# A new written order, and GpSimd compute operations that each wait for the one before

## The chip, the cores and the metric

One core of a Trainium2 chip runs the kernel. Its engines are TensorE (PE; its weight loads are listed as PEld), VectorE (DVE), ScalarE (ACT), GpSimd (POOL) and SyncE (SP, which here only issues transfers). The metric is the time of one execution in device microseconds. Before the change it is 179.48 us, the median of three runs from 178.18 to 181.58.

## The reference, cut to what matters

```
state = 0                                   # per batch (4) and head (8), 48 x 48
for t in range(768):
    cur    = (u * k[t]) outer v[t]
    y[t]   = r[t] @ (state + cur)
    state  = w * state + k[t] outer v[t]

x     = y as (4, 768, 384)
u     = x + real(fft(fft(x, axis=1), axis=2))
un    = (u - mean(u)) / sqrt(var(u) + 1e-6)   # over the 384 columns
out   = u + relu(un @ w_ch1) @ w_ch2          # 384 -> 1536 -> 384
```

## The kernel before, in words

The recurrence is done in 24 chunks of 128 time steps, six for each of the four batches. For a chunk, k and r are scaled with powers of w (`KR`, line 386 for one half, 389 for both at once), transposed on TensorE (line 410) and copied to `KRT` (lines 420, 421). Their product `PR` (432, 434) gives the diagonal term, the scores (444) are copied (`AC`, 451) and masked (`MA`: on GpSimd at 453, on VectorE at 456). `y` is then summed on TensorE (508, 514, 535) and leaves as `X` (543, 545). The state runs along the chunks (475, 488, 490).

When a batch has its six `X`, sums and differences of it are formed that fold the two transforms: `HH` and `XF` chunk by chunk in batch 0 (lines 558, 561, 567), `EO`, `HH` and `XF` for the whole batch in batches 1 to 3 (586, 594, 603). The first transform multiplies `XF` with a table (line 636), the second follows at 677. Then come `UF` (689), the statistics, the normalised `UB` (696 to 701) and its transpose `UNT`. The two matrix products of the last step run in eight halves of a batch: line 765 into `HT` (770 on ScalarE, 771 on VectorE), line 786 into `osb` (796), which is stored.

Nothing is scheduled when the kernel runs or is built. All steps stand in a list, and `ORDER` is a written sequence of their numbers; a suffix such as `.1` chooses among the engines on which a step may run, or leaves a step out. `emit` goes through that sequence, gives each new tile the buffer of its ring that was free longest, and issues the step. So the sequence sets, for every engine and for the transfer queues of SP and POOL, which instruction stands behind which. Among the steps are matmuls on a tile of zeros (line 272, and 366) whose results nobody uses; `ORDER` takes in as many as it names.

GpSimd issues its own transfers as well: the four parts of `wuc` (302), the two weight tables (840, 843) and part of the stores (799). They stand in its queue among its compute operations.

Of the kernel before, what the change touches and what calls it, by code (L numbers as in the profile page):

```python
# [9 lines left out]
AluOp = mybir.AluOpType  # L10
# [5 lines left out]
H = 8  # L16
S = 768
D = 48
# [43 lines left out]
class _Schedule:  # L62
# [12 lines left out]
    def emit(self, order):  # L75
        last = {}
        for k, (n, a) in enumerate(order):
            o = self.ops[n]
            for t in o["new"] + o["use"] + o["uses"][a]:
                last[t] = k  # L80
        held = {name: [-1] * len(tiles) for name, tiles in self.rings.items()}
        for k, (n, a) in enumerate(order):
            o = self.ops[n]
            for t in o["new"]:
                ends = held[t.ring]
                m = min(range(len(ends)), key=ends.__getitem__)
                assert ends[m] < k, (o["name"], t.ring)
                ends[m] = last[t]
                t.value = self.rings[t.ring][m] if t.view is None else t.view(self.rings[t.ring][m])
            fn = o["alts"][a][2]  # L90
            if fn is not None:
                fn()
# [78 lines left out]
def kernel(  # L171
# [19 lines left out]
    sch = _Schedule()  # L191
# [690 lines left out]
```

## Time and profile before

| what | value |
|---|---|
| median of three runs | 179.48 us (178.18 to 181.58) |
| the profiled execution | 177.02 us, span 175.3 us |
| TensorE busy | 157.2 us, 90% of the span |
| VectorE busy | 138.7 us, 79% |
| ScalarE busy | 108.4 us, 62% |
| GpSimd busy | 80.8 us, 46% |

The span runs from the first to the last instruction of the profiled execution; its own time is 1.72 us longer. Busy shares are means over stretches that have different limits, so the table by stretch among the rows below tells more than this one. A busy TensorE is not TensorE at its peak, since matmuls overlap.

### The profile page before, as it was taken

The page shows a single profiled execution, that of the slowest core. Times are in us where ns is not written, and L with a number is a line of the kernel's source. Part 1 is how long each engine was busy: PE and PEld are TensorE (multiplying, and loading weights), DVE is VectorE, ACT ScalarE, POOL GpSimd, SP SyncE. Part 2 cuts the span into 40 slices and gives each one's busy share as a digit, 9 for nine tenths or more (in the row PEclk, how much of TensorE's full clock was granted, in tenths as well). Part 3 has the DMA queues.
Part 4 walks back from the last instruction along what each step waited for, and adds up shares of the span by engine and source line. Part 5 has one row for each costly group of instructions (what it writes and reads, how often), then busy time and mean ns, then how long its engine had stood idle before and what let it go on. Part 6 is the DMA issues. An engine that isn't in the chain of part 4 may idle for free. (4 is left out here: it accounts for less than half of the span.)

```text
span 175.3 us, 4260 instructions
## 1 busy us (share of the span) xinstructions
PE 157.2 (90%) x1589; PEld 111.8 (64%) x1590; DVE 138.7 (79%) x314; ACT 108.4 (62%) x260; POOL 80.8 (46%) x120
## 2 busy tenths in 40 slices
PE   6348989829999979999999899999999999999992
PEld 1136667627777756677666478667676876666661
DVE  5487999999988979999979998868899775511632
ACT  2375889528868995578996266957735770275210
POOL 6606947693776640466974453473452121020110
PEclk9999999999999999999999999999999999999999
DMA  5999989799099999999999989999500043420132
GB/s 117 219 202 212 245 166 221 181 186 175 2 184 177 203 212 201 186 238 138 213 199 230 267 174 244 187 138 227 152 0 0 4 121 81 112 95 0 45 124 100
DMA packets 98118, 27.08 MB, mean 155 GB/s; under 512 B 94369, under 2 KB 96930, under 8 KB 98098
## 3 DMA queue, kind: packets, MB, share of 16 engines
q1 hardware_dynamic: 92912, 21.70, 63.2%
q0 software_dynamic: 2064, 4.53, 11.0%
q10 hardware_dynamic: 3122, 0.59, 2.1%
q8 instruction: 12, 0.20, 0.5%
q14 instruction: 8, 0.07, 0.1%
HBM read 19.77 MB, written 4.72 MB: 140 GB/s over the span
## 5 line engine op out<-in xcount | busy, mean ns | idle before, releaser
L765 PE MATMUL bank<-UNT,W 128*128 128x384 bf16 x288 | 54.4, 326 | 0.0
L786 PE MATMUL bank<-W,HT 128*128 128x384 bf16 x276 | 51.9, 326 | 0.9 <-DMA W<-in_moe_w_ch_dram 0.9
L770 ACT ACTIVATE HT<-bank 128x384 bf16<-128x384 f32 x68 | 30.6, 494 | 27.2 <-PE bank L765 27.0
L765 PEld LDWEIGHTS <-W 128*128 128x128 bf16 x288 | 30.6, 114 | 11.5 <-DMA UNT<-UB 0.2
L786 PEld LDWEIGHTS <-HT 128*128 128x128 bf16 x276 | 25.9, 98 | 15.7 <-DMA W<-in_moe_w_ch_dram 1.1
L453 POOL TENSOR_SCALAR_AFFINE_SELECT MA<-AC 128x512 bf16<-128x512 bf16 x25 | 17.3, 701 | 10.8 <-ACT AC L451 8.4
L796 DVE SCALAR_TENSOR_TENSOR osb<-bank,rstd,UF 128x384 f32<-128x384 f32 x23 | 13.9, 614 | 9.3 <-PE bank L786 9.1
L386 POOL TENSOR_TENSOR KR<-kr,wtab 128x384 bf16<-128x384 f32 x15 | 16.5, 1106 | 7.3 <-DMA kr<-in_r_dram 5.4
L771 DVE TENSOR_SCALAR HT<-bank 128x384 bf16<-128x384 f32 x28 | 15.0, 552 | 6.1 <-PE bank L765 6.0
L386 DVE TENSOR_TENSOR KR<-kr,wtab 128x384 bf16<-128x384 f32 x29 | 16.5, 586 | 3.1 <-ACT wtab L326 2.8
L451 ACT CAST AC<-bank 128x512 bf16<-128x512 f32 x25 | 14.2, 586 | 4.1 <-PE bank L444 2.0
L799 POOL DMA_DIRECT2D out_dram<-osb x11 | 6.3, 568 | 22.0 <-DVE osb L796 19.9
L636 PE MATMUL bank<-te_t,XF 128*128 128x193 bf16 x108 | 12.2, 247 | 4.5 <-DVE XF L567 3.8
L456 DVE TENSOR_TENSOR MA<-bank,mtri 128x512 bf16<-128x512 f32 x23 | 15.4, 683 | 0.7 <-PE bank L444 0.6
L708 ACT ACTIVATE tn_t<-UF,sm 128x384 bf16<-128x384 f32 x24 | 14.8, 617 | 0.2
L410 PE MATMUL bank<-ident,KR 128*128 128x128 bf16 x112 | 12.0, 251 | 3.0 <-DVE KR L386 2.8
L432 POOL TENSOR_TENSOR PR<-KRT 128x512 bf16<-128x512 bf16 x9 | 10.4, 1156 | 7.3 <-ACT KRT L420 4.1
L636 PEld LDWEIGHTS <-XF 128*128 128x128 bf16 x120 | 9.9, 97 | 5.7 <-DVE XF L567 4.0
L689 DVE SCALAR_TENSOR_TENSOR UF<-bank,X 128x384 f32<-128x384 f32 x22 | 11.6, 548 | 1.7 <-PE bank L677 1.7
L410 PEld LDWEIGHTS <-KR 128*128 128x128 bf16 x112 | 8.8, 113 | 5.8 <-issue 3.5
L523 DVE TENSOR_TENSOR TT<-V,bank 128x384 bf16<-128x384 bf16 x19 | 10.3, 544 | 2.6 <-PE bank L514 2.5
L543 DVE TENSOR_TENSOR X<-bank,TT 128x384 bf16<-128x384 f32 x18 | 9.6, 550 | 2.4 <-PE bank L535 2.4
(108 smaller groups left out, 263.8 us busy)
## 6 DMA issues: line engine op xcount, KB each, us to landing
kr<-in_k_dram SPq DMA_DIRECT2D x23, 192.0 KB, 4.2
kr<-in_r_dram SPq DMA_DIRECT2D x23, 192.0 KB, 4.4
vt<-in_v_dram SPq DMA_DIRECT2D x23, 192.0 KB, 4.3
out_dram<-osb SPq DMA_DIRECT2D x12, 192.0 KB, 1.9
out_dram<-osb POOLq DMA_DIRECT2D x11, 192.0 KB, 3.1
W<-in_moe_w_ch_dram POOLq DMA_DIRECT2D x2, 576.0 KB, 7.5
W<-in_moe_w_ch_dram POOLq DMA_DIRECT2D x3, 384.0 KB, 6.2
te_t<-te_c SPq DMA_DIRECT2D x1, 579.0 KB, 5.4
```

What stands on the lines that cost most here:

```text
L386: eng.tensor_tensor(out=o, in0=x, in1=y, op=AluOp.mult)
L410: nc.tensor.transpose(tps[s]()[:, p, :], KR()[:, s, p, :], ident)
L451: op(("AC", i, a), [("ACT", "AC", lambda: nc.scalar.copy(AC(), A_ps[a]())), ("NONE", "", None)], r=[("A", i)], w=[("AC", i, a)], new=[AC], ...
L453: op(("MA", i, a), [("POOL", "MA", lambda: nc.gpsimd.affine_select(out=MA[a](), in_=AC(), pattern=[[0, NP], [1, 128]], base=0, channel_mul ...
L456: ("DVE", "MA", lambda: nc.vector.tensor_tensor(out=MA[a](), in0=A_ps[a](), in1=mtri.unsqueeze(1).to_broadcast([128, NP, 128]), op=AluOp.m ...
L636: nc.tensor.matmul(fp()[:, par, :], lhsT=lhsT[:, g * CH:g * CH + 128], rhs=rhs, start=(nb == 0 and par == 0), stop=(nb == last and par == ...
L708: ("ACT", "SQ", lambda: nc.scalar.activation(out=squares, in_=UF()[:, j, :], func=Act.Square, scale=-float(DM), bias=sm()[:, j:j + 1], acc ...
L765: nc.tensor.matmul(hp(), lhsT=W1[:, dt, ft // 4 * 512 + ft % 4:(ft // 4 + 1) * 512:4], rhs=UNT()[:, :, dt, :], start=(dt == 0), stop=(dt = ...
L770: op(("HT", hf, ft), [("ACT", "HT", lambda: nc.scalar.activation(out=HT()[:, ft, :], in_=hp(), func=Act.Relu, scale=-1.0)), ("DVE", "HT", ...
L771: ("DVE", "HT", lambda: nc.vector.tensor_scalar(out=HT()[:, ft, :], in0=hp(), scalar1=-1.0, scalar2=0.0, op0=AluOp.mult, op1=AluOp.max))],
L786: nc.tensor.matmul(mo(), lhsT=HT()[:, ft, j * 128:(j + 1) * 128], rhs=W2[:, ft, :], start=(ft == 0), stop=(ft == 11))
L796: one(("osb", hf, j), "DVE", "osb", lambda: nc.vector.scalar_tensor_tensor(out=osb(), in0=mo(), scalar=rstd()[:, j:j + 1], in1=UF()[:, j, ...
```

## The change: what it does

`ORDER` is another sequence over the same steps, with other choices of engine. `emit` now hands every compute instruction that it issues on GpSimd (not its transfers) to `chain`, which makes it wait for the completion of the preceding compute instruction there. Three helper functions return the instruction that they make so that this can be done. Nothing else changes; from the steps' definitions on, line numbers are higher by 11.

```diff
-            fn = o["alts"][a][2]
+            eng, key, fn = o["alts"][a]
             if fn is not None:
-                fn()
+                made = fn()
+                if eng == "POOL" and not key.startswith("dma"):
+                    self.chain(made)
...
 ORDER = """
-152 15 159 158 28 150 160 46 151 174 155 164 8 165 173.1 196 193 202 32 34 199.1 205 203 153 208 176 181 200.1 154 182
+155 159 152 202 30 203 150 158 151 168 208 172 205 206 154 211 209 173 164 199.1 163 165 200.1 181.1 179 162 161 201.1
...
+    before = []
+
+    def chain(made):
+        if before:
+            tc.add_manual_dep(made.ins, before[-1].ins.name,
+                              mybir.DependencyInfo(mybir.DependencyClass.Sync, mybir.DependencyReason.DATA),
+                              reason="all cores of GpSimd done")
+        before.append(made)
+
+    sch.chain = chain
...
-            eng.tensor_tensor(out=o, in0=x, in1=y, op=AluOp.mult)
+            return eng.tensor_tensor(out=o, in0=x, in1=y, op=AluOp.mult)
...
-            eng.tensor_tensor(out=TT(), in0=V(), in1=x.unsqueeze(2).to_broadcast([128, H, D]), op=AluOp.mult)
+            return eng.tensor_tensor(out=TT(), in0=V(), in1=x.unsqueeze(2).to_broadcast([128, H, D]), op=AluOp.mult)
...
-                eng.tensor_copy(TR()[0:97, 2 * g:2 * g + 2, :], TT()[0:97, 2 * g:2 * g + 2, 384:0:-1])
+                return eng.tensor_copy(TR()[0:97, 2 * g:2 * g + 2, :], TT()[0:97, 2 * g:2 * g + 2, 384:0:-1])
```

On GpSimd 99 instructions now wait for GpSimd itself, where 11 did. The counts that change most, before and after: masks `MA` 25 and 31 on GpSimd, 23 and 17 on VectorE; `HT` 28 and 23 on VectorE, 68 and 73 on ScalarE; half products `KR` 15 and 17 on GpSimd, 29 and 25 on VectorE, with 2 and 3 whole ones there; matmuls on zeros 11 and 10.

The first place is GpSimd's queue while the last sums of batch 0 are formed, around the two transfers of the first weight table (`W`, the rows with DMA). Before:

```order
L567 TENSOR_TENSOR XF_100<-HH_99 128x196
L558 TENSOR_TENSOR HH_99<-X_142 128x192
L386 TENSOR_TENSOR KR_91<-kr_102,wtab_78 128x8x48
L567 TENSOR_TENSOR XF_100<-HH_99 128x2x98
L840 DMA W_88<-in_moe_w_ch_dram 128x3x768
L386 TENSOR_TENSOR KR_90<-kr_104,wtab_79 128x8x48
L432 TENSOR_TENSOR PR_126<-KRT_122 128x512
L840 DMA W_88<-in_moe_w_ch_dram 128x3x768
L386 TENSOR_TENSOR KR_92<-kr_105,wtab_77 128x8x48
L403 CAST V_117<-vt_109 128x384
```

And now:

```order
L578 TENSOR_TENSOR XF_100<-HH_99 128x2x98
L569 TENSOR_TENSOR HH_99<-X_142 128x192
L578 TENSOR_TENSOR XF_100<-HH_99 128x2x98
L851 DMA W_88<-in_moe_w_ch_dram 128x3x768
L578 TENSOR_TENSOR XF_100<-HH_99 128x2x98
L851 DMA W_88<-in_moe_w_ch_dram 128x3x768
L464 AFFINE_SELECT MA_132<-AC_128 128x512
L397 TENSOR_TENSOR KR_93<-kr_103,wtab_77 128x8x48
L666 COPY TR_147<-TT_145 97x768
L443 TENSOR_TENSOR PR_123<-KRT_121 128x512
```

Three `XF` now lie at the two transfers where one did, and the product `KR` and `PR` between the transfers are gone from there.

The second place is VectorE from the last `X` of batch 1 to the `XF` of batch 1 for which TensorE's first transform waits. Before:

```order
L543 TENSOR_TENSOR X_143<-bank_63,TT_139 128x384
L386 TENSOR_TENSOR KR_92<-kr_104,wtab_78 128x8x48
L543 TENSOR_TENSOR X_142<-bank_64,TT_141 128x384
L586 TENSOR_TENSOR EO_144<-X_143 128x768
L586 TENSOR_TENSOR EO_144<-X_143 128x384
L386 TENSOR_TENSOR KR_92<-kr_104,wtab_78 128x8x48
L586 TENSOR_TENSOR EO_144<-X_143 128x768
L586 TENSOR_TENSOR EO_144<-X_143 128x384
L594 TENSOR_TENSOR HH_99<-EO_144 128x2x2x192
L594 TENSOR_TENSOR HH_99<-EO_144 128x2x192
L594 TENSOR_TENSOR HH_99<-EO_144 128x2x2x192
L603 TENSOR_TENSOR XF_101<-HH_99 128x2x3x98 x4
```

And now:

```order
L597 TENSOR_TENSOR EO_144<-X_143 128x768
L534 TENSOR_TENSOR TT_141<-V_115,bank_66 128x384
L753 RECIPROCAL rstd_171<-rstd_171 128x3
L605 TENSOR_TENSOR HH_99<-EO_144 128x2x2x192
L554 TENSOR_TENSOR X_143<-bank_66,TT_141 128x384
L605 TENSOR_TENSOR HH_99<-EO_144 128x2x2x192
L397 TENSOR_TENSOR KR_93<-kr_104,wtab_78 128x8x48
L597 TENSOR_TENSOR EO_144<-X_143 128x384 x2
L605 TENSOR_TENSOR HH_99<-EO_144 128x2x192 x2
L614 TENSOR_TENSOR XF_101<-HH_99 128x2x3x98 x4
```

The two large `EO` and one `HH` now stand ahead of the last `X` of the batch. On TensorE there are 45 matmuls of line 786 between that chunk's sum `y` and the first transform before, and 27 (now line 797) after; at the same place of batch 2 there are 45 of lines 765 and 786 before and 39 after.

## Rows read from the trace of the kernel before

**Rows 1.** The page: busy time of each engine over the span.
```profile
PE 157.2 (90%) x1589; PEld 111.8 (64%) x1590; DVE 138.7 (79%) x314; ACT 108.4 (62%) x260; POOL 80.8 (46%) x120
```

**Rows 2.** Busy time by stretch: bounds and length, engines, granted clock, DMA share, GB/s.
```profile
35.00:40.00 5.00, 1.87 (x26) 1.72 (x24) 5.00 (x5) 1.49 (x4) 4.70 (x6) 1.00 1.11 189
...
60.00:65.00 5.00, 4.06 (x60) 2.79 (x59) 4.07 (x9) 4.85 (x11) 2.66 (x5) 1.00 1.02 189
...
100.00:105.00 5.00, 4.40 (x38) 3.43 (x39) 4.91 (x12) 2.49 (x5) 2.28 (x2) 1.00 0.94 185
...
120.00:125.00 5.00, 4.88 (x72) 3.43 (x70) 3.75 (x9) 3.87 (x11) 1.78 (x3) 1.00 1.00 238
...
165.00:170.00 5.00, 5.00 (x35) 3.21 (x34) 1.97 (x5) 1.76 (x5) 1.08 (x2) 1.00 0.21 79
```

**Rows 3.** Timeline of PE: start, length, instruction, idle before it and its releaser.
```profile
38.16 0.26 PE L636 MATMUL bank<-te_t,XF 128*128 128x193 bf16 x1 [3.13 <-DVE XF L567]
```

**Rows 4.** Timeline of DVE, 32 to 38 us: an undisturbed XF and a long one.
```profile
32.21 0.25 DVE L567 TENSOR_TENSOR XF<-HH 128x196 bf16<-128x196 bf16 x1
...
34.45 3.18 DVE L567 TENSOR_TENSOR XF<-HH 128x196 bf16<-128x196 bf16 x1
```

**Rows 5.** Timeline of POOL, 34 to 38 us.
```profile
34.23 0.80 POOL L840 DMA_DIRECT2D W<-in_moe_w_ch_dram  x1
35.05 1.00 POOL L386 TENSOR_TENSOR KR<-kr,wtab 128x384 bf16<-128x384 f32 x1
36.00 1.15 POOL L432 TENSOR_TENSOR PR<-KRT 128x512 bf16<-128x512 bf16 x1
```

**Rows 6.** Timeline, 125.7 to 128.8 us: POOL with DVE's PR between.
```profile
125.78 0.82 POOL L523 TENSOR_TENSOR TT<-V,DE 128x384 bf16<-128x384 bf16 x1
126.29 0.59 DVE L432 TENSOR_TENSOR PR<-KRT 128x512 bf16<-128x512 bf16 x1
126.77 0.63 POOL L453 TENSOR_SCALAR_AFFINE_SELECT MA<-AC 128x512 bf16<-128x512 bf16 x1 [0.17 <-ACT AC L451]
...
127.36 0.50 POOL L403 CAST V<-vt 128x384 bf16<-128x384 f32 x1
127.94 0.83 POOL L523 TENSOR_TENSOR TT<-V,DE 128x384 bf16<-128x384 bf16 x1
```

**Rows 7.** Timeline at the start: DVE's icol and the last of POOL's six memsets.
```profile
2.56 2.07 DVE L304 CAST icol<-icol_i 128x3 f32<-128x3 int32 x1 [1.23 <-POOL icol_i L288]
...
4.28 0.32 POOL L310 MEMSET KR<- 128x256 bf16 x1
```

**Rows 8.** Timeline, 91 to 101 us: PE, then DVE.
```profile
97.83 2.11 PE L786 MATMUL bank<-W,HT 128*128 128x384 bf16 x12
100.47 1.74 PE L636 MATMUL bank<-te_t,XF 128*128 128x193 bf16 x15 [0.53 <-DVE XF L603]
...
94.73 4.35 DVE L594 TENSOR_TENSOR HH<-EO 128x768 bf16<-128x768 bf16 x3
99.18 1.62 DVE L603 TENSOR_TENSOR XF<-HH 128x588 bf16<-128x588 bf16 x4
```

**Rows 9.** Timeline of DVE, 65 to 73 us, then of PE at 71 us.
```profile
65.31 1.02 DVE L543 TENSOR_TENSOR X<-bank,TT 128x384 bf16<-128x384 f32 x2 [1.03 <-PE bank L535]
...
67.18 0.82 DVE L586 TENSOR_TENSOR EO<-X 128x768 bf16<-128x768 bf16 x2
...
69.12 1.56 DVE L594 TENSOR_TENSOR HH<-EO 128x768 bf16<-128x768 bf16 x4
70.71 1.92 DVE L603 TENSOR_TENSOR XF<-HH 128x588 bf16<-128x588 bf16 x4
...
71.26 2.61 PE L786 MATMUL bank<-W,HT 128*128 128x384 bf16 x15
```

**Rows 10.** The page: costliest groups, busy, mean ns of one, idle before.
```profile
L453 POOL TENSOR_SCALAR_AFFINE_SELECT MA<-AC 128x512 bf16<-128x512 bf16 x25 | 17.3, 701 | 10.8 <-ACT AC L451 8.4
...
L386 POOL TENSOR_TENSOR KR<-kr,wtab 128x384 bf16<-128x384 f32 x15 | 16.5, 1106 | 7.3 <-DMA kr<-in_r_dram 5.4
```

123 rows, old and new, of the table ORDER are left out of this document.

## The prediction

> **What bounds the kernel now.** The page comes first: TensorE is busy for 157.2 of 175.3 us, far more than any other engine [rows 1], so time can only come out of its idle 18 us, or be lost by adding to them. The table by stretch says where those are. From 45 us on it is busy in practically every microsecond (5.00 of 5 us, as in the stretch from 165 to 170) [rows 2]; before that it is VectorE that is full (5.00 of 5 us from 35 to 40) while TensorE has 1.87. So up to about 45 us the kernel goes at the pace of VectorE and of what it waits for, and afterwards at TensorE's.
>
> The timeline of TensorE names the largest gap: 3.13 us in the first transform of batch 0, ended by an `XF` of VectorE [rows 3]. From 45 to 170 us three stretches are not full and lack 0.94, 0.60 and 0.12 us [rows 2], 1.7 in all; 0.53 of it is for `XF` of batch 2 [rows 8].
>
> Why was `XF` late? Undisturbed it takes 0.25 us, but one took 3.18 [rows 4]. Beside it GpSimd issues a transfer and does a `KR` and a `PR`; the long `XF` ends at 37.63, after `PR` has ended at 37.15 [rows 5]. GpSimd's `KR` and `PR` overlap: 35.05 + 1.00 is 36.05, and `PR` starts at 36.00. VectorE stood through both. The same is seen twice more: the little `icol` took 2.07 us and ended at 4.63, just after the last memset of GpSimd's run, at 4.60 [rows 7]; three `HH` took 4.35 us [rows 8], against 1.56 us for four [rows 9]. Where GpSimd paused for 0.17 us (126.60 to 126.77) a waiting `PR` got through: it ended at 126.88, and GpSimd's next instruction kept its 0.63 us [rows 6].
>
> **The change part by part.** All sums are against the profiled execution, 177.02 us.
>
> *The wait on GpSimd.* Its price shows where `TT` needs the `V` cast directly before it: `V` ends at 127.86, `TT` starts at 127.94, a gap of 0.08 us [rows 6], where neighbours otherwise overlap by 0.05 [rows 5]. So 0.13 us for each pair that stood back to back. With 99 waits, that is at most 12.9 us on GpSimd and at least nothing, since its other waits cover the rest. Its own work grows by about 8 us: six masks at 0.70 and two `KR` at 1.11 make 6.4 [rows 10], and the remaining exchanges some 1.5. From 80.8 us it comes to between 89 and 102, up to 58% of the span. Behind a waiting instruction on that queue stand masks that `y` needs, `UB`, and transfers. After 45 us TensorE has other work in its order to cover that. Before 45 us GpSimd gives sums and masks to a stretch without cover; some 27 waits there are 0 to 3.5 us. I take 0.5, near the low end, because GpSimd's masks had 10.8 us of idle time before them anyway, 8.4 of it waiting for ScalarE's copy [rows 10]. **+0.5 us (0 to +3.5).**
>
> *The last sums of batch 0.* Up to the last `XF` of batch 0 VectorE has nearly the same list of instructions in both orders, by number and kind; so mainly its delays can change. What stood between the two transfers, `KR` and `PR`, is replaced by one `XF` that GpSimd itself does, and the instructions after the second transfer now have a pause between them. The delay of 2.93 us (3.18 less 0.25) [rows 4] should shrink to about one GpSimd instruction, 1.0 to 1.2 us [rows 5]: 1.7 less. Against it, if the pause of 0.08 us lets nobody in, nothing is gained; if it works as at 126.6, all 2.9 are. I take the middle, since the pause that was seen to work was twice as long. **-1.7 us (-2.9 to 0).** The next thing late would then be GpSimd's own `XF`, which waits behind a weight transfer of 0.80 us.
>
> *The start.* `icol` can gain up to 1.9 us, as GpSimd's memsets no longer form one run. But VectorE now has more memsets ahead of what the first matmul needs, and the first `KR` is made in one piece, from two tables instead of one at a time: about 1.0 us later relative to the tables. **0 us (-0.9 to +1.0).** Three of the six early matmuls on zeros also go. The granted clock reads 1.00 in all stretches [rows 2], TensorE does not bound this stretch, and I set 0, with +1 at the outside.
>
> *Ahead of the first transforms of batches 1 and 2.* Batch 1: from the last `y` to the transform TensorE has 27 table matmuls instead of 45. Fifteen take 2.45 us (2.61 less the tail that overlaps) [rows 9], so 27 take 4.4, and with four transposes and two groups of scores 5.3 us. VectorE has, from the last `X`: `X` 0.5, one large `HH` 0.5, `KR` 0.5, two small `EO` 0.6, two small `HH` 0.6, four `XF` 1.6 to 1.9 [rows 8, 9]: 4.3 to 4.6 us. Slack 0.7. Batch 2: 39 matmuls, 6.3 us, against `X` 0.5, four `EO` 1.6, four `HH` 1.6, a reciprocal 0.1, four `XF` 1.6 to 1.9: 5.4 to 5.7. Slack 0.6. Each bears one short delay by GpSimd, not two. Before, batch 2 had 45 matmuls, lost about 3 us on `HH`, and 0.53 us of that reached TensorE [rows 8]. Of the 1.7 us that were idle after 45 us I expect 0.3 at each of these two places and 0.5 elsewhere. **-0.6 us (-1.3 to +3.7).**
>
> *The rest.* VectorE loses about 5 us of work (six masks, five `HT`), which after 45 us nobody waits for while TensorE is full: 0. TensorE's own work is unchanged but for a few matmuls: 0. At the end two stores move to GpSimd, hidden by matmuls that still follow: 0 to +0.5.
>
> The sum: 0.5 - 1.7 + 0 - 0.6 = -1.8, so 175.2 us for an execution like the profiled one. The median shown is 2.46 us above that execution; I carry the difference along: **177.7 us**.
>
> A rule that speaks against part of this: the Trainium skill, page "SBUF — State Buffer", section "Who interferes with whom", says that a VectorE instruction with two SBUF inputs and a GpSimd instruction that reads SBUF exclude each other, and that the later one is held until the first has finished, thus through one instruction. By that rule the wait on GpSimd would free VectorE of nothing, and what the second term gives would come from the moved rows alone. Rows 4 and 5 differ from it: VectorE was held past the end of a first instruction and through a second.
>
> **The rivals.**
>
> *The pause works everywhere (faster).* Every wait of VectorE ends with the GpSimd instruction during which it began. For it: three long holds end exactly with GpSimd's runs [rows 4, 5, 7, 8]. Against: the pause is 0.08 us, only 0.17 is seen to work, and transfers are not chained, so a run of transfer and compute keeps its form. Then -2.9 at the sums, -0.9 at the start, -1.3 later and nothing lost: -5.1, a median of 174.4.
>
> *GpSimd sets the pace up to 45 us (no change).* It already has 4.70 of 5 us from 35 to 40 [rows 2]; the waits and the added `KR` and masks cost some 4.9 us there, of which 2 to 3 reach the first normalised rows. With the other terms, 2.5 - 1.7 - 0.6 = +0.2: 179.7.
>
> *The thin cover breaks (slower).* In batches 1 and 2 VectorE's `HH` or `XF` meet a run of GpSimd as at 94.73 [rows 8]: 3.1 us each time, less 0.7 and 0.6 of slack, so 4.9 us of TensorE idle. For it: GpSimd has `KR` for the next batch in its queue there. Against: these are now chained. With no gain at batch 0, 0.5 for the waits, 0.5 of other idle, and the old 1.7 gone, the sum is +4.2: 183.7. It decides from the second such run on; a single one gives no change.
>
> *The long hold was not GpSimd's doing,* and the wait changes nothing for VectorE: then only the price of the wait and the later places count, 0.5 - 0.6 = -0.1: 179.4.
>
> **How the numbers follow.** Two per cent, about what a measurement of this kernel can tell from no change (its three runs spread over 1.9%), is 3.6 us: faster is under 175.9, slower over 183.1. Chances: the forecast 0.40, all pauses work 0.24, GpSimd sets the pace 0.13, no effect on VectorE 0.10, thin cover 0.13. The forecast's own bounds reach a little below 175.9 and a little of the first rival stays above it, so faster 0.26; slower is the last rival with a bit of the unknown start, 0.14; within 2% the remaining 0.60. The range reaches down to the first rival's 174.4 and up to 182.0, which leaves out most of the slower case and the best end of the faster one.
>
> **What would show it right or wrong.** Right: the idle time ahead of batch 0's first transform falls from 3.13 us to 1 to 2; no VectorE instruction is held through two chained GpSimd instructions; GpSimd's neighbours stand 0.08 us apart; idle time of TensorE from 45 us to its last matmul is near 1.1 us (before: 1.7). Wrong: a long `XF` or `HH` beside chained instructions (the pause lets nobody in), idle TensorE of over 1 us ahead of the transforms of batches 1 or 2 (cover), or TensorE waiting for GpSimd's `XF`, masks or `UB` before 45 us (pace). Should the first matrix product begin later than 47 us, the start or GpSimd was mis-sized.

## The result and the profile after

The changed kernel takes 173.35 us (median of four runs, 172.38 to 173.67), the kernel before 179.21 us beside it (four runs, 178.18 to 181.58). The ratio is 0.968, with a 95% interval from 0.962 to 0.975: faster. A second comparison, below, gave 0.976 (0.973 to 0.980). Ratios are meant for undisturbed executions, without those that are over 1.5% longer than the shortest of their kernel; medians and ranges have all of them. Forecast were 177.7 us, in a range from 174.4 to 182.0; the result lies below the range.

The profiled execution of the changed kernel takes 173.32 us with a span of 171.6: 3.70 us less than before. Its page answers to [rows 1]: less work for VectorE, more for GpSimd, TensorE nearly as before.

```profile
PE 156.2 (91%) x1591; PEld 111.5 (65%) x1591; DVE 127.8 (74%) x310; ACT 109.7 (64%) x259; POOL 92.3 (54%) x128
```

The table by stretch answers to [rows 2], with three more stretches:

```profile
20.00:25.00 5.00, 3.80 (x60) 2.96 (x60) 4.99 (x10) 4.69 (x12) 3.99 (x7) 0.82 1.02 197
25.00:30.00 5.00, 4.49 (x64) 3.31 (x63) 4.96 (x13) 4.35 (x9) 3.82 (x5) 0.83 1.00 253
35.00:40.00 5.00, 4.93 (x68) 3.79 (x67) 5.00 (x11) 4.22 (x10) 4.68 (x6) 1.00 1.03 167
40.00:45.00 5.00, 3.47 (x54) 2.69 (x53) 3.82 (x12) 3.90 (x11) 4.43 (x7) 1.00 1.05 192
60.00:65.00 5.00, 5.00 (x45) 3.30 (x44) 2.99 (x9) 3.79 (x11) 1.87 (x3) 1.00 1.42 151
100.00:105.00 5.00, 5.00 (x46) 3.92 (x43) 3.61 (x11) 3.74 (x8) 3.23 (x4) 1.00 1.06 208
120.00:125.00 5.00, 5.00 (x56) 3.60 (x55) 4.90 (x11) 3.41 (x10) 4.70 (x7) 1.00 0.37 112
```

From 35 to 40 us TensorE has 4.93 us of work where it had 1.87; the three later stretches that were short are full. New is a hole from 40 to 45 us, and a granted clock of 0.82 and 0.83 from 20 to 30.

At the last sums of batch 0, VectorE answers to [rows 4] and GpSimd to [rows 5]:

```profile
34.49 0.26 DVE L578 TENSOR_TENSOR XF<-HH 128x196 bf16<-128x196 bf16 x1 [0.73 <-POOL XF L578]
34.67 0.99 DVE L397 TENSOR_TENSOR KR<-kr,wtab 128x384 bf16<-128x384 f32 x1
```
```profile
33.94 0.52 POOL L578 TENSOR_TENSOR XF<-HH 128x196 bf16<-128x196 bf16 x1
34.40 0.79 POOL L851 DMA_DIRECT2D W<-in_moe_w_ch_dram  x1
35.20 0.96 POOL L464 TENSOR_SCALAR_AFFINE_SELECT MA<-AC 128x512 bf16<-128x512 bf16 x1
36.23 1.00 POOL L397 TENSOR_TENSOR KR<-kr,wtab 128x384 bf16<-128x384 f32 x1
37.30 1.05 POOL L666 COPY TR<-TT 97x768 bf16<-97x768 bf16 x1
38.43 1.16 POOL L443 TENSOR_TENSOR PR<-KRT 128x512 bf16<-128x512 bf16 x1
```

`XF` takes 0.26 us, and TensorE has no gap ahead of or in the first transform (before 3.13 us, [rows 3]). GpSimd's neighbours stand 0.07 and 0.08 us apart (36.23 + 1.00 to 37.30, 37.30 + 1.05 to 38.43). VectorE's `KR`, which starts while the second transfer is issued (34.40 to 35.19), takes 0.46 us more than its next one (0.53 us).

At the start, VectorE's `icol` (before [rows 7]) and TensorE's first transposes:

```profile
1.66 0.39 DVE L315 CAST icol<-icol_i 128x3 f32<-128x3 int32 x1
```
```profile
8.47 1.90 PE L421 MATMUL bank<-ident,KR 128*128 128x128 bf16 x16 [3.74 <-DVE KR L400]
```

The transposes began at 9.18 us before. And the hole, on TensorE:

```profile
43.06 0.33 PE L776 MATMUL bank<-UNT,W 128*128 128x384 bf16 x1
44.70 1.49 PE L776 MATMUL bank<-UNT,W 128*128 128x384 bf16 x8 [1.31 <-DMA W<-in_moe_w_ch_dram]
```

One matmul of the first matrix product runs, then 1.31 us are lost to a weight transfer. Its end, 44.70, is where the second transfer (issued at 34.40) lands after 10.3 us, though these products need columns of the first alone, which had landed at 41.3. This fits a dependency that is taken over the whole stretch of memory that a transfer spans: with both halves interleaved in `W1[dt][F]` the second one spans the columns of `dt` 1 and 2 too, and the one matmul that ran reads `dt` 0, which lies ahead of that stretch. The thirds and halves below test it.

How far the changed kernel is ahead, by the useful matmul columns that TensorE still has to do (at each time of the old execution, when the new one had as many left):

```
old execution, us     20    36    40    46    48    68    100   140   last matmul   span
new one earlier by    1.2   1.1   4.2   4.7   2.6   3.7   3.1   4.1   4.1           3.7
```

So 1.1 us from the start, 3.1 at the gap, 0.5 up to 46, 2.1 lost again around the weight transfer, 1.5 gained later, 0.4 lost behind the last matmul. A second trace of the changed kernel (at the end of the weight transfers, below) differs from this one by up to 0.7 us on the way, so smaller differences between two traces tell little.

### The profile page after: what moved, and what is told of

Its sections match the earlier page's. It is cut to its first block, busy times and chain, and to the rows that moved or that the text cites. A ratio compares the mean times of both kernels' runs of the same rounds, so it can differ in the third digit from the quotient of the medians.

```text
span 171.6 us, 4305 instructions
## 1 busy us (share of the span) xinstructions
PE 156.2 (91%) x1591; PEld 111.5 (65%) x1591; DVE 127.8 (74%) x310; ACT 109.7 (64%) x259; POOL 92.3 (54%) x128
## 4 chain that ended last, share of the span: by engine, by line
PE 58%; DMA 12%; POOL 11%; DVE 6%; issue 6%; ACT 4%; POOLq 0%; DVEq 0%; ACTq 0%
PE bank L776 24%; PE bank L797 21%; DMA W<-in_moe_w_ch_dram 6%; POOL KR L397 3%; DMA wuc<-in_w_dram 3%; DMA KRT<-KR 3%; PE bank L647 2%; PE bank L688 2%; PE bank L455 2%; POOL MA L464 2%; PE bank L546 2%; POOL UB L712 1%; DVE TT L534 1%; PE bank L823 1%; POOL PR L443 1%
## 5 line engine op out<-in xcount | busy, mean ns | idle before, releaser
L781 ACT ACTIVATE HT<-bank 128x384 bf16<-128x384 f32 x73 | 33.1, 495 | 29.0 <-PE bank L776 28.8
L464 POOL TENSOR_SCALAR_AFFINE_SELECT MA<-AC 128x512 bf16<-128x512 bf16 x31 | 21.4, 690 | 14.3 <-issue 6.9
L810 POOL DMA_DIRECT2D out_dram<-osb x14 | 8.0, 571 | 28.2 <-DVE rstd L753 18.1
L397 POOL TENSOR_TENSOR KR<-kr,wtab 128x384 bf16<-128x384 f32 x17 | 19.1, 1124 | 6.8 <-ACT wtab L337 4.1
L462 ACT CAST AC<-bank 128x512 bf16<-128x512 f32 x31 | 17.7, 593 | 6.2 <-PE bank L455 2.8
L782 DVE TENSOR_SCALAR HT<-bank 128x384 bf16<-128x384 f32 x23 | 12.3, 551 | 7.9 <-PE bank L776 5.9
L719 ACT ACTIVATE tn_t<-UF,sm 128x384 bf16<-128x384 f32 x21 | 13.1, 623 | 1.2 <-DVE UF L700 1.1
L534 DVE TENSOR_TENSOR TT<-V,bank 128x384 bf16<-128x384 bf16 x21 | 11.4, 548 | 2.7 <-ACT AC L462 1.2
L455 PE MATMUL bank<-KRT 64*128 64x128 bf16 x192 | 10.2, 229 | 2.0 <-ACT KRT L431 0.6
L467 DVE TENSOR_TENSOR MA<-bank,mtri 128x512 bf16<-128x512 f32 x17 | 11.4, 682 | 0.6 <-PE bank L455 0.6
```

The source lines that it names most:

```text
L397: return eng.tensor_tensor(out=o, in0=x, in1=y, op=AluOp.mult)
L455: nc.tensor.matmul(A_ps[a]()[:, p, :], lhsT=KRT()[rows, 0, p, :], rhs=QT(p, rows), start=(p == 0), stop=(p == NP - 1), skip_group_check=True)
L462: op(("AC", i, a), [("ACT", "AC", lambda: nc.scalar.copy(AC(), A_ps[a]())), ("NONE", "", None)], r=[("A", i)], w=[("AC", i, a)], new=[AC], ...
L464: op(("MA", i, a), [("POOL", "MA", lambda: nc.gpsimd.affine_select(out=MA[a](), in_=AC(), pattern=[[0, NP], [1, 128]], base=0, channel_mul ...
L534: return eng.tensor_tensor(out=TT(), in0=V(), in1=x.unsqueeze(2).to_broadcast([128, H, D]), op=AluOp.mult)
L719: ("ACT", "SQ", lambda: nc.scalar.activation(out=squares, in_=UF()[:, j, :], func=Act.Square, scale=-float(DM), bias=sm()[:, j:j + 1], acc ...
```

## The experiments

**The order alone, and the wait alone.** The first leaves the two lines out that call `chain`; the second has the changed code with the old `ORDER`.

```diff
-                if eng == "POOL" and not key.startswith("dma"):
-                    self.chain(made)
```

> The new order without the waits on GpSimd. Theory one (the waits let VectorE in, and the order uses that): without them GpSimd's neighbours overlap again, VectorE is held through two or three of them in several places, its holds together grow by some 4 to 8 us, and the time goes back by 1.5 to 3 us, to 175 to 177 us. Rival (the order alone does it, the waits only cost): the time stays at 173.4 or falls by up to 1 us, since 88 waits at 0.08 to 0.13 us leave GpSimd; VectorE's holds stay as they are.

> The old order with the waits. Theory one: the XF that took 3.18 us in the old kernel takes 1.2 to 2.0 us, the gap ahead of batch 0's first transform falls from 3.13 to 1 to 2 us, the run of three HH of 4.35 us shrinks to about 2.5, and the time falls by 1.5 to 3 us, to 176 to 178 us. Rival (the order alone): XF stays above 2.7 us, or another instruction is held instead, and the time stays within 1 us of 179.2 or rises by the price of the waits before 45 us, 0.5 to 3.5 us.

Order alone: 175.59 us, ratio 0.985 (0.978 to 0.992). Wait alone: 175.99 us, ratio 0.987 (0.975 to 1.000). By these ratios each gives about 1.4% and both together 3.2 (2.4 in the second comparison). That they simply add is not shown, for the wait alone scatters as the kernel before does: its four executions take 173.42, 175.01, 176.96 and 178.62 us, and its ratio evidently has the long ones in it, for the two shorter ones are 2.3% below the kernel before. The shortest has the trace, and is as short as the changed kernel: its transposes begin 1.32 us earlier than before, its gap is 1.45 us, and its last matmul ends 3.6 us earlier (4.1 in the changed kernel). TensorE and VectorE of the wait alone:

```profile
35.25 0.26 PE L648 MATMUL bank<-te_t,XF 128*128 128x193 bf16 x1 [1.45 <-DVE XF L579]
```
```profile
91.53 3.96 DVE L606 TENSOR_TENSOR HH<-EO 128x768 bf16<-128x768 bf16 x3
```

The run of three `HH` (4.35 us, [rows 8]) stays long, where 2.5 was expected: GpSimd's two `KR` there alternate with transfers, which aren't chained. In the changed kernel `HH` of this size take 0.55 us on average.

That the order does it alone is out: its four executions (175.2 to 176.0) lie above all ten of the changed kernel's (172.4 to 173.9). At the start it needs no waits: its `icol` takes 0.39 us as well, and its transposes begin at 8.28. It is up to 0.5 us ahead of the changed kernel from 28 to 34 us, which may be the price of the waits, and 2.5 behind it at 38: without the waits the loss moves one instruction on. VectorE, GpSimd and TensorE of the order alone:

```profile
37.49 2.64 DVE L395 TENSOR_TENSOR KR<-kr,wtab 128x384 bf16<-128x384 f32 x1
```
```profile
36.83 0.81 POOL L664 COPY TR<-TT 97x768 bf16<-97x768 bf16 x1
37.62 1.14 POOL L441 TENSOR_TENSOR PR<-KRT 128x512 bf16<-128x512 bf16 x1
38.73 0.98 POOL L395 TENSOR_TENSOR KR<-kr,wtab 128x384 bf16<-128x384 f32 x1
```
```profile
40.19 0.62 PE L419 MATMUL bank<-ident,KR 128*128 128x128 bf16 x8 [2.02 <-DVE KR L395]
```

`XF` is free, but the next `KR`, 0.53 us in the changed kernel at this place, is held for 2.1 us through three overlapping instructions, and TensorE stands for 2.02 us. Behind that gap the granted clock falls to 0.50, half speed (stretches of 1 us, columns as before):

```profile
42.00:43.00 1.00, 1.00 (x9) 0.83 (x7) 1.00 (x4) 0.00 (x0) 0.58 (x1) 0.50 1.18 216
43.00:44.00 1.00, 1.00 (x8) 0.92 (x7) 0.53 (x4) 0.74 (x3) 0.05 (x1) 0.50 1.10 220
```

**One wait, and the waits of the start.** Old order; `chain` waits at one place alone (`PR` behind `KR`, between the two transfers), or among GpSimd's first twelve compute instructions.

```diff
-        if before:
+        if len(before) == 31:                 # the one wait
+        if before and len(before) < 12:       # the waits of the start
```

> The old order with a single wait: GpSimd's PR between the two weight transfers waits for the KR ahead of it. Theory one (a pause of 0.08 us is enough for VectorE): the XF that took 3.18 us ends with KR, about 1.7 us, the gap of 3.13 us ahead of batch 0's first transform falls by 1.2 to 1.5 us, and the time falls by as much, a ratio of 0.992. Rival (the pause is too short, or the next held instruction takes back the gain): XF stays over 2.7 us or a KR or HH of VectorE behind it is held by PR for as long; the gap stays above 2.7 us and the ratio is 1.00.

> The old order with the waits only among GpSimd's first twelve compute instructions (memsets and masks of the start), none later. Theory one (the pauses let icol through): icol takes 0.4 to 0.5 us instead of 2.07, the first transposes begin at 7.9 instead of 9.18 us, and all later events up to the long XF are 1.3 us earlier; the XF is held as before (2.9 us); the time falls by 1.3 us, a ratio of 0.993. Rival (the start is waited for by nobody, because the loads land later anyway): icol is short, but from 20 us on the lead is under 0.3 us and the ratio is 1.00.

One wait: 175.06 us, ratio 0.988 (0.983 to 0.993), by the ratios as much as all 84 added ones give in that order (0.987), though the wide interval of those leaves room for more. VectorE, GpSimd and TensorE of this kernel, to be held against [rows 3 to 5]:

```profile
33.87 1.74 DVE L579 TENSOR_TENSOR XF<-HH 128x196 bf16<-128x196 bf16 x1
```
```profile
33.66 0.80 POOL L852 DMA_DIRECT2D W<-in_moe_w_ch_dram  x1
34.47 1.00 POOL L398 TENSOR_TENSOR KR<-kr,wtab 128x384 bf16<-128x384 f32 x1
35.55 1.24 POOL L444 TENSOR_TENSOR PR<-KRT 128x512 bf16<-128x512 bf16 x1
```
```profile
35.84 0.26 PE L648 MATMUL bank<-te_t,XF 128*128 128x193 bf16 x1 [1.38 <-DVE XF L579]
```

A pause of 0.08 us (34.47 + 1.00 to 35.55) lets VectorE in: `XF` falls from 3.18 to 1.74 us, the gap from 3.13 to 1.38. The transfer ahead of `KR` isn't chained, and through these two `XF` is still held. By the Trainium skill, page "SBUF — State Buffer", section "Who interferes with whom", as the forecast read it, the wait would free VectorE of nothing; here it freed it of 1.44 us, so the measurement decides against that reading.

The waits of the start: 176.58 us, ratio 0.995 (0.991 to 0.999). VectorE and TensorE:

```profile
2.56 0.47 DVE L316 CAST icol<-icol_i 128x3 f32<-128x3 int32 x1 [1.23 <-POOL icol_i L300]
```
```profile
7.86 1.03 PE L422 MATMUL bank<-ident,KR 128*128 128x128 bf16 x8 [1.91 <-DVE KR L398]
...
36.69 0.26 PE L648 MATMUL bank<-te_t,XF 128*128 128x193 bf16 x1 [3.13 <-DVE XF L579]
```

`icol` takes 0.47 us instead of 2.07, the transposes begin 1.32 us earlier, and the lead is still 1.47 us at 36.69, where the old gap of 3.13 us ends. Then some 0.8 of it are lost: here the clock falls behind the gap, which it didn't in the first profile.

```profile
38.00:39.00 1.00, 1.00 (x9) 0.94 (x8) 1.00 (x3) 0.23 (x2) 0.27 (x1) 0.50 1.15 204
39.00:40.00 1.00, 1.00 (x20) 0.89 (x17) 1.00 (x3) 1.00 (x2) 0.00 (x0) 0.50 1.25 234
```

**The clock of 0.82.** Nine matmuls on zeros more in three gaps of TensorE at 17, 20 and 22 us (nine of the unused numbers of `idle` in `ORDER`).

> The changed kernel with nine more matmuls on zeros in three gaps of TensorE of 1.10, 0.78 and 0.60 us at 17, 20 and 22 us. In the changed kernel the granted clock reads 0.82 and 0.83 from 20 to 30 us, and four transposes that take 0.38 us at 16.6 and 20.6 us take 0.63 at 24.5 and 25.9. Theory one (the clock costs time): the clock reads 1.00 in both stretches, the work from 23 to 26.4 us takes some 1.3 us less, and the time falls by 0.5 to 1.5 us. Rival (VectorE sets the pace there: 4.99 and 4.96 of 5 us busy): the clock comes back, the time stays within 0.3 us.

175.10 us, ratio 0.981 (0.972 to 0.989): not faster, against both expectations, for in its profile TensorE is 1.0 us later than in the changed kernel at 30 us and 1.5 at the end. The zeros took longer than the gaps they were put in (1.62 and 0.92 us in the first two, of 1.10 and 0.78) and delayed what others wait for, so this run alone doesn't price the clock, which did come back:

```profile
20.00:25.00 5.00, 3.57 (x49) 1.99 (x47) 3.32 (x8) 4.09 (x10) 3.84 (x6) 1.00 0.96 189
25.00:30.00 5.00, 4.21 (x68) 3.04 (x70) 4.97 (x12) 4.47 (x10) 3.36 (x5) 1.00 1.03 249
```

The next kernels do: in the profiles of the weights ahead and of the thirds the clock reads 1.00 there without added zeros, and at 30 us they stand 0.2 us ahead of the changed kernel and 0.3 us behind it, which is within what two traces of one kernel differ by. VectorE, with 4.99 and 4.96 of 5 us, sets the pace.

**The weight transfers.** First earlier, then in thirds that lie apart, then in halves that lie apart; last the loads of the start.

```diff
-... 550.1 464 573.2 346 ... 1010
-1308 1011 516 490 ... 479.1 1309 495
+... 550.1 464 1308 573.2 346 ... 1010
+1011 1309 516 490 ... 479.1 495
```

> The changed kernel with the two transfers of the first weight table issued earlier by GpSimd: the first behind the two masks of chunk 5 (where GpSimd was idle for 1.49 us), the second where the first stood. In the changed kernel the first matrix product stops after one matmul for 1.31 us, for this transfer, which landed 10.7 us after its issue. Theory one: the wait goes wholly, the time falls by 1.3 us, to about 172.1. Rival: the transfer only shares its 16 engines with the loads of k, r and v, which then come late, or its issue of 0.8 us holds GpSimd's XF and VectorE: the time stays at 173.4 or rises by up to 1 us.

173.24 us, ratio 0.973 (0.965 to 0.982): no gain, as the rival had it. The wait at the product goes, but `k` of a later chunk lands later: VectorE waits 1.22 us for it, and TensorE for VectorE. The trace is of the longest of its four executions (174.81 us, the others 172.60 to 173.29); whether those have this wait is not shown.

```profile
39.01 0.95 DVE L397 TENSOR_TENSOR KR<-kr,wtab 128x384 bf16<-128x384 f32 x1 [1.22 <-DMA kr<-in_k_dram]
```
```profile
40.02 0.62 PE L421 MATMUL bank<-ident,KR 128*128 128x128 bf16 x8 [1.67 <-DVE KR L397]
```

```diff
-    W1 = const([128, 3, F], BF16, "W1")
+    W1 = const([128, 3, 3, 512], BF16, "W1")
-lhsT=W1[:, dt, ft // 4 * 512 + ft % 4:(ft // 4 + 1) * 512:4]
+lhsT=W1[:, ft // 4, dt, ft % 4:512:4]
```

> The changed kernel with the first weight table kept as three thirds that lie apart (W1[n][dt][512 columns]) and fetched in three transfers, the first third first, the other two behind the place of the second transfer. In the changed kernel TensorE waits 1.31 us at its second matrix product until 44.70 us, which is the landing of the second transfer (issued at 34.40, 10.3 us) although the product needs only the first. Theory one (the wait is for the wrong half): the wait goes, the products begin at some 43.0 us and run on, TensorE is 1.3 us earlier from there to the end, about 172. Rival: the products then wait for ScalarE's copies or for the other thirds a little later, and most of the 1.3 us comes back before 50 us: 173 to 173.5; or the third transfer costs GpSimd 0.6 us at 35 us and delays its KR and TR: no gain.

172.57 us, ratio 0.975 (0.969 to 0.982). The products begin at 43.97 us and run without a wait while the last third is still on its way (issued at 35.47, landing 10.0 us later), so it was the wrong half that was waited for. The third transfer costs 1.02 us of it, in GpSimd's queue ahead of `TR`:

```profile
39.33 1.17 PE L688 MATMUL bank<-hid_t,TR 97*128 97x192 bf16 x12 [1.02 <-POOL TR L666]
...
43.97 1.62 PE L776 MATMUL bank<-UNT,W 128*128 128x384 bf16 x9
```

```diff
+    W1 = const([128, 2, 3, 768], BF16, "W1")
+lhsT=W1[:, ft // 6, dt, ft % 6:768:6]
-            out=W2[:, n * 4:(n + 1) * 4, :], in_=w2[n * 512:(n + 1) * 512, :].rearrange("(p f) d -> p f d", f=4)))
+            out=W2[:, n * 6:(n + 1) * 6, :], in_=w2[n * 768:(n + 1) * 768, :].rearrange("(p f) d -> p f d", f=6)))
```

> The changed kernel with the two halves of the first weight table apart in memory (W1[n][dt][768 columns], its columns dealt out six by six instead of four by four, and the second table's rows to match, in two transfers instead of three), so that a product on the first half needs only the first transfer and GpSimd issues no more transfers than before. With thirds the wait of 1.31 us went, but TR stood 1.02 us behind the third transfer. Theory one: both go, the products begin at 43.0 us without a wait, and the end comes 1.3 us earlier than the changed kernel on the same chip: a ratio of 0.992 to it, 0.961 to the kernel before. Rival: the second half, which lands at 44.7 us, is then waited for at the tenth product (some 44.8 us), or ScalarE's and VectorE's copies HT become the bound, and under 0.4 us are gained.

173.64 us, ratio 0.978 (0.974 to 0.982). No wait at the first table is left, and the first nine products run while the second half is still on its way (it lands at 45.3 us). But the second table's first half is now larger and is waited for, and 0.84 us are lost to ScalarE right after:

```profile
43.53 1.64 PE L776 MATMUL bank<-UNT,W 128*128 128x384 bf16 x9
...
59.85 0.66 PE L797 MATMUL bank<-W,HT 128*128 128x384 bf16 x3 [0.44 <-DMA W<-in_moe_w_ch_dram]
61.36 0.40 PE L421 MATMUL bank<-ident,KR 128*128 128x128 bf16 x4 [0.84 <-ACT HT L781]
```

```diff
-187 184 185 166 169.1 170.1 186 274 275 276
+184 185 166 169.1 170.1 274 275 276 187 186
 (and chunk 0's r on SP, ahead of the other loads)
```

> The changed kernel with chunk 0's r fetched first on SP instead of third on ScalarE's queue, and the two tables of chunk 0 made before those of chunk 1. In the changed kernel the first KR starts at 7.46 us, when ScalarE's third and fourth tables end (6.92 and 7.42) and r of chunk 0 lands (issued at 1.85, landing after 5.5). Theory one (the start carries through to the end, as the wait alone at the start seems to do): the first transposes come at 7.4 to 7.6 instead of 8.47 us and the end 0.8 to 1.0 us earlier, about 172.4. Rival: the loads of chunks 1 to 4 come later in turn, VectorE and GpSimd wait for them, and TensorE stands where it did from 15 us on: 173.4 within 0.4.

172.35 us, ratio 0.974 (0.970 to 0.979). The transposes begin at 7.54 instead of 8.47 us, but 0.3 us of that are left from 28 to 44 us: VectorE's pace in between takes it back. The trace still ends 1.1 us ahead of the changed kernel's, 0.6 of it because the wait at the weight table is 0.71 us in this execution. So the time that was expected came, but mostly not from the start.

> The halves apart, and chunk 0's r fetched first with its tables made first. Theory one (the two gains lie in different stretches and add: 0.3 us were carried from the start to 44 us in the kernel with the first loads, 1.3 us come at the products): 1.6 us less than the changed kernel, a ratio of 0.991 to it, 0.959 to the kernel before, about 171.7. Rival: what is earlier at 43 us meets the transfers of the weights, which land when they do: the sum is no better than the halves alone.

> The changed kernel once more, on the chip of the two others, to compare them with. Expected: the ratio of 0.968 to the kernel before, within its interval of 0.962 to 0.975, and the same idle places of TensorE: 1.31 us ahead of the second matrix product, none over 0.3 us from 30 to 42 us. Should it come out under 0.962 or over 0.975, the first result was a matter of the chip.

Both together: 174.21 us, ratio 0.978 (0.972 to 0.983), no better than the halves alone, as the rival had it. The changed kernel beside them: 173.66 us, ratio 0.976 (0.973 to 0.980), on a chip where the kernel before took 177.74. That is outside the 0.962 to 0.975 that were expected: the changed kernel took 0.3 us more than in the first comparison, the kernel before 1.5 less. The first table's wait was 0.41 us there, not 1.31. So none of these five versions can be told from the changed kernel, and no better one was found.

**Why the kernel before scatters.** Three more executions of it, for their traces.

> The old kernel once more, unchanged, for its trace. Its executions scatter from 175.8 to 182.0 us, the changed kernel's from 172.4 to 173.9. Theory one (the gap of 3.13 us has a second price): in an execution that is longer than the one profiled first, the granted clock reads 0.50 for some us behind that gap or behind another long idle time of TensorE, as it did in the old order with waits at the start (0.50 and 0.65 from 37 to 41 us) and in the new order without waits (0.50 from 42 to 45 us); the extra time is there, 1 to 3 us. Rival: the extra time lies at the start (loads that land later) or at transfers, and the clock reads 1.00 behind the gap.

> The same kernel and the same question, another execution: theory one finds the extra time of any execution over 177.5 us behind the gap of 3.13 us, with a granted clock of 0.50 there; the rival finds it at the start or at transfers, with the clock at 1.00.

> The same kernel and the same question, a third execution: theory one finds the extra time of any execution over 177.5 us behind the gap of 3.13 us, with a granted clock of 0.50 there; the rival finds it at the start or at transfers, with the clock at 1.00.

181.08, 179.39 and 176.66 us, against the 177.02 of the first profile. All three have the gap of 3.13 us, and in all three the clock falls behind it (0.76 to 0.91 in the stretch from 40 to 45 us, where the first profile had 1.00). That costs 0.7 to 0.9 us. The larger part of the two long ones lies at 60 to 68 us: there GpSimd's in-order queue waits for a load, and TensorE for its `V` behind it. GpSimd, TensorE and the stretch of the longest:

```profile
65.27 0.50 POOL L403 CAST V<-vt 128x384 bf16<-128x384 f32 x1 [7.04 <-DMA vt<-in_v_dram]
```
```profile
65.82 0.33 PE L475 MATMUL bank<-V,KR 128*128 128x96 bf16 x4 [1.99 <-POOL V L403]
```
```profile
65.00:70.00 5.00, 3.87 (x38) 2.46 (x38) 2.42 (x5) 3.19 (x8) 2.62 (x5) 0.66 0.99 181
```

In the first profile the same `V` waited 0.91 us. Over the first profile the longest execution loses 2.9 us here and 1.0 more up to 76 us, partly at a fallen clock. So theory and rival are both right, each for a part. In the new order this `V` isn't GpSimd's at that place, and the gap is gone; the changed kernel's ten timed executions lie within 1.5 us. The new order isn't free of long executions, though: with the halves apart, alone and with the loads, the longest took 177.16 and 177.14 us, and have no trace. That those two places make up all of the scatter is not shown: other executions have no trace.

## Why the prediction was wrong, step by step

- **The wait on GpSimd, +0.5.** As priced, as far as can be told: neighbours stand 0.07 to 0.08 us apart, GpSimd's busy time is 92.3 us (89 to 102 expected), and the kernel without waits is up to 0.5 us ahead from 28 to 34 us, which is within what two traces of one kernel differ by.
- **The last sums of batch 0, -1.7 (-2.9 to 0).** The gap went wholly: -3.1. For the wait by itself 1.7 was right: one wait took 1.75 us off the gap. The step failed in taking the old queue's rows for it: the rows moved between the transfers do the rest for `XF`, and the wait then keeps the next `KR` from being held (2.02 us of TensorE without it). That GpSimd's own `XF` would be next to come late proved true (0.73 us of VectorE), but TensorE had other work. The reading that the holds end exactly with GpSimd's runs was loose for `XF`: it ended 0.48 us behind `PR` [rows 4, 5], longer than its own 0.25.
- **The start, 0 (-0.9 to +1.0).** It gave -0.7 at the transposes and -1.1 at 36 us. The failed step is the set-off of 1.0 us for the whole `KR` and the memsets. The first `KR` starts 1.02 us earlier (7.46, before 8.48), and the transposes follow it after 1.01 us instead of 0.70, so the set-off measures 0.3. The moved rows do this without the waits; the waits alone, in the old order, gave -1.3.
- **Batches 1 and 2, -0.6 (-1.3 to +3.7).** No idle time at either transform. Of the 1.7 us idle after 45 us about 0.5 is left; -1.5 by the count of columns. Some 1.1 of that come from 60 to 65 us, where the first profile waits 0.9 us for the second weight table, whose transfers the new order issues 4 to 8 us earlier; that was not a step of its own. No run changes the sums of batches 1 and 2 alone, so what their new places are worth is not shown.
- **The rest, 0.** Two parts failed. Around the first weight table about 2.1 us of the lead go from 46 to 48 us; where 0.8 of them went is not shown, and 1.31 are a wait that no step had asked for: the product moved forward from 46.86 to 43.06 us, to where its transfer had not landed. Behind the last matmul 0.4 us are lost, within the bound given.
- **The difference of 2.46 us, carried along.** The largest miss after all: the changed kernel's median is 0.03 us above its profile. The difference came from three executions; over 17 and 11 later ones, on other chips, the median of the kernel before is 177.57 and 177.74 us, 0.55 and 0.72 above its profile. So it was no constant of the measurement. In the long executions that have a trace it is what the old kernel loses behind the gap and at a load, which its first profile does not show, or shows shorter.

The sum of the profile was -3.7 where -1.8 stood; with the 2.46 this is the miss of 4.35 us. Nearest was the rival in which every pause works, at 174.4; its terms for the gap, the start and the later places (-2.9, -0.9, -1.3) came out at -3.1, -1.1 and -1.5. That its time came near is luck all the same: its sum of -5.1 is 1.4 too much, and the 2.46 that it carried along took that back. How much its ground, the pause by itself, carries stays open: by the ratio of the wait alone about half, by its one trace nearly all (3.6 of 4.1 us).

## What to carry to other kernels

Where two engines exclude each other, look for instructions that stand back to back without a wait on the one that isn't the bound: a wait of 0.08 us there can be worth 1.4 us on the other, and it may need to stand only where someone is held (one wait did most of it at the gap; the new order was not tried with so few). A median that lies above its profile is a term of its own: find the waits of the long executions before carrying the difference along. And when work is moved forward, ask of each of its transfers when it lands, and whether the dependency asks for more than the data it reads.

## What was not expected of the hardware

After the same gap of 3.13 us the granted clock stayed at 1.00 in one execution and fell in four others (to 0.50, or 1.2 instead of 2.4 GHz, for some 3 us where it was read by the microsecond), at a cost of 0.7 to 0.9 us; what decides it is not shown. So a gap of TensorE has a second price that a single profile may not show. A clock of 0.82 over 10 us, on the other hand, cost nothing that two traces could tell (0.3 us) where VectorE was full.
